# Attention output stored once in fp32 and split where it is used, and the recalled memory scaled behind the reads of the third score tile

## The chip, the cores and the metric

One core of a Trainium2 chip runs the whole program. The metric is device time in microseconds (us) from start to end of one execution; a kernel's time is the median of three runs.

## What is computed

Attention with a memory, then a gated MoE layer, all in fp32 (B 4, H 8, S 576, D 64; 2304 tokens, d 512, ff 1536):

```python
a = softmax(causal(q @ k.T / 8))
local = a @ v
mem_out = (phi(q) @ M_prev) / (phi(q) @ z_prev + 1e-6)      # phi(x) = elu(x) + 1
x = sigmoid(beta) * mem_out + (1 - sigmoid(beta)) * local     # 2304 x 512
out = (silu(x @ w_gate) * (x @ w_val)) @ w_out
```

## The kernel before

**Parts of fp32.** A matmul operand in fp32 is a sum of two fp32r tiles, a high part (a cast) and a low part (the number less its high part), and a product takes three matmuls: high x high, high x low, low x high. Where this text speaks of a split, it means a cast on ScalarE and a subtraction on VectorE or GpSimd.

**Attention** runs in iterations n = 0 to 16, one for each of the 16 (batch, pair of heads), the loop `for n in range(NP + 1)`. Iteration n computes scores, maxima and exponentials of pair n (`cur`) and the turned probabilities, the product with v and the memory part of pair n - 1 (`old`); it also splits q and k of pair n + 1 (`after`). Iteration 16 has no scores, it only finishes pair 15. Scores come in tiles of 128 queries t = 0 to 3 for each of two heads, and a last one of 64 queries for both (two halves of 288 keys, "the fourth-block scores"). All engines run in program order: the helper `queued` records every operation at L84 and ties it to the one before on its engine, so the order of the Python code is the order on each engine.

In an iteration VectorE reads the score tiles (`reading`, a custom reduction that adds a mask, scales, and takes the maximum `mx`; out tiles `ps` for t = 0, 1, `pl` for t = 2, 3, `p` for the last), makes the reciprocals `rs` of the sums `sm`, copies turned tiles (`g`), and scales the recalled memory: `mem = tr * w`, two operations in `recall`'s `scale()`. ScalarE computes the exponentials. GpSimd (`pool`) casts q and k of the next pair (`kh`, `qh`), makes their low parts (`ql`, `kl`), and multiplies the probabilities by `rs` and the gate `og`: four `ps`, four `pl` and one `p` for each pair, in `weighed`. A bank of scores is written again only when VectorE has read it.

At the end of an iteration the output of pair n - 1 stands in two PSUM tiles `tr`, 256 and 320 wide. `give` splits each out of PSUM: ScalarE casts it to `xh`, VectorE writes `xl = tr - xh`. The 256-wide one is done at the end of the iteration, the 320-wide one behind the first scores of the next; then two DMAs (`d2`) store `xh` and `xl` to DRAM, `xdh` and `xdl`. I call the start of the scores of iteration n boundary n. In iterations 3 to 15 three thirds of a weight matrix are prepared at the boundaries, one operation of VectorE each (from `EARLY` = 2, 6, 10): a clamp (`we`) at boundaries 4, 8, 12, a move (`wa`) at 5, 9, 13, a word (`wa`, two inputs of 512) at 6, 10, 14 and a low part (`wgl`, `wol`) at 7, 11, 15.

**MoE.** Tokens come in three blocks of 768 (`ORDER`), ff in 12 slices: 36 units. Each half block of x is 384 tokens. The first three units are plain (`eight`); the others take seven products in Strassen's manner (`seven`) from sums of quarters of x: `p1`, `p2`, `p4` and `p7`, `p6`, `p5`, `p3`, each with a high and a low tile `xp1h`, `xp1l` and so on. Products use two PSUM banks (`s`) in turn, so product n + 2 of a unit waits until VectorE or ScalarE has taken product n. `weigh` forms the products of gate and value, `zg` (i = 0) and `zh` (i = 1), and their splits `uh`, `ul`; `lower` multiplies the `u` of the unit before with w_out. `operands` prepares the weights of the next unit (`tt`, `bl`, `tl`). `plan[k]` lists what VectorE and ScalarE do behind product k of a unit. `sums(t0)` makes the sums of a block: it loads four quarters from `xdh` and `xdl` into `xr`, adds high and low (four additions 128x768), and forms s1, s and the two differences (four more). `direct` loads `p1`, `p2`, `p4` (for block 0 also `p7`) as they are, high and low, by DMA. For block 1 the sums stand in units 6 to 11 of block 0, for block 2 in units 9 to 11 of block 1.

Of the kernel before, what the change touches and what calls it, by code (L numbers as in the profile page):

```python
# [44 lines left out]
def attention_moe(ctx: ExitStack, tc: tile.TileContext, qt, kt_, v, m, beta, wg, wv, wo, out):  # L45
# [9 lines left out]
    xdh = dram.tile([128, NPAIR, NT], F32, name="xdh")  # L55
    xdl = dram.tile([128, NPAIR, NT], F32, name="xdl")
# [109 lines left out]
    xs = {p: [near.tile([128, 2, N2], F32R, name=f"x{p}{part}") for part in "hl"] for p in ("p1", "p2", "p7", "p4")}  # L166

# [88 lines left out]
    with tc.tile_pool(name="sb", bufs=1, reuse_waits="tile") as sb:  # L256
# [69 lines left out]
        class Pair:  # L326
# [181 lines left out]
            def give(self, t0, src):  # L508
                c = slice(t0 * 128, t0 * 128 + src.shape[1])
                act.copy(self.xh[:, c], src)  # L510
                return lambda: dve.tensor_tensor(self.xl[:, c], src, self.xh[:, c].bitcast(F32), op=ALU.subtract)

# [28 lines left out]
            def leave(self):  # L541
                first, rest = self.av
                self.xh = rot(sb, "xh", [128, 576], F32R, NX)
                self.xl = rot(sb, "xl", [128, 576], F32R, NX)
                self.give(0, first[:, 0:256])()

                def ending():
                    low = self.give(2, rest[:, 0:320])
                    return lambda: (low(), self.d2())

                return ending

            def d2(self):
                for dst, src in ((xdh, self.xh), (xdl, self.xl)):
                    SP.dma_start(dst[:, self.pr, self.b * S : self.b * S + S], src.bitcast(F32))
# [10 lines left out]
        ending = lambda: nothing  # L566
        copies = []
        for n in range(NP + 1):
# [10 lines left out]
            low = ending()  # L579
# [5 lines left out]
            low()  # L585
# [32 lines left out]
            scale()  # L618
# [6 lines left out]
            reads[0](1)  # L625
            if n == 0:
                one_less()
                scaled()
# [37 lines left out]
            ending = old.leave() if old else lambda: nothing  # L666
# [5 lines left out]
            for i, at in enumerate(EARLY):  # L672
                if n == at:
                    raw_top(act, i)
                if n == at + 1 and i < 3:
                    third_clamp(dve, i)
                if n == at + 2 and i < 3:
                    third_move(dve, i)
                if n == at + 3 and i < 3:
                    third_word(act, dve, i, copies)  # L680
                if n == at + 4 and i < 3:
                    low_part(dve)
            if n in AHEAD:
                raw_load(AHEAD.index(n), loads.get(n + 2))

        ending()()
# [7 lines left out]
    with tc.tile_pool(name="stg2", bufs=1, reuse_waits="tile") as stg2, \  # L694
# [47 lines left out]
        def block(x, t0, i, j):  # L742
            return x[:, 2 * j : 2 * j + 2, t0 + i * N2 : t0 + i * N2 + N2]

        def direct(t0, p, i, j):
            for dst, src in zip(xs[p], (xdh, xdl)):
                SP.dma_start(dst.bitcast(F32), block(src, t0, i, j))

        def sums(t0, here=False):

            got = rot(mbp, "xr", [128, 4, 2, N2], F32, 1)
            at = ((1, 0), (1, 1), (0, 0), (0, 1))
            a21, a22, a11, a12 = (got[:, n] for n in range(4))
            s1, s = (rot(mbp, name, [128, 2, N2], F32, 1) for name in ("xt", "xm"))
            tmp = (s, s1)
            mix = dict(p6=s, p7=a11, p5=s1, p3=a12)

            def load(n):
                for dst, src in ((got[:, n], xdh), (tmp[n % 2], xdl)):
                    ld = SP.dma_start(dst, block(src, t0, *at[n]))  # L760
                    follow(ld, last[DVE], "the loads that come before go first", mybir.DependencyClass.Sync)

            def add(n):
                if here:
                    h, l = (x.bitcast(F32) for x in xs[("p7", "p4", "p1", "p2")[n]])
                    dve.tensor_tensor(got[:, n], h, l, op=ALU.add)
                    return
                dve.tensor_tensor(got[:, n], got[:, n], tmp[n % 2], op=ALU.add)
                if n + 2 < 4:
                    load(n + 2)  # L770

            tt = lambda out, a, b, op: (lambda: dve.tensor_tensor(out, a, b, op=op))
            work = [lambda n=n: add(n) for n in range(4)] + [
                tt(s1, a21, a22, ALU.add), tt(s, s1, a11, ALU.subtract), tt(a12, a12, s, ALU.subtract),
                tt(a11, a11, a21, ALU.subtract),
            ]
            return lambda: (load(0), load(1)), work, mix
# [137 lines left out]
        first = units[0][0]  # L915
        for p, i, j in (("p1", 0, 0), ("p2", 0, 1), ("p7", 1, 0), ("p4", 1, 1)):
            direct(first, p, i, j)
# [5 lines left out]
        for n, unit in enumerate(units):  # L923
# [23 lines left out]
            if plain:  # L947
                if f == 0:
                    _, due, mix = sums(t0, True)
                    for k, some_ in enumerate(((0,), (1,), (2, 4), (3,))):  # L950
                        plan[k] += [due[i] for i in some_]
                if f == 1:
                    for k in range(3):
                        plan[k].append(due[5 + k])
                    for k, p in ((0, "p5"), (2, "p6")):
                        plan[k] += spreads(mix, ("h", p))
# [5 lines left out]
            if not end:  # L962
                follows = ORDER[ORDER.index(t0) + 1]
                if t0 == first and left in (5, 4, 3):
                    if left == 5:
                        begin, due, mix = sums(follows)
                        begin()
                    plan[5].append(due[5 - left])
                if not plain:
                    if left == 3 and t0 != first:  # L970
                        begin, due, mix = sums(follows)
                        plan[3].append(begin)
                    if left == 2:
                        for k, work in zip((5,), due[3:]) if t0 == first else zip((2, 4, 6), due):
                            plan[k].append(work)
                    if left == 1:
                        for k, work in zip((1, 3, 5), due[4:]) if t0 == first else zip((1, 2, 4, 6), due[3:]):
                            plan[k].append(work)
                    if left == 0:
                        plan[2].append(due[7])  # L980
                        plan[3] += spreads(mix, ("h", "p6"))
                        plan[4] += spreads(mix, ("l", "p6"), ("h", "p7"))
                        plan[6] += spreads(mix, ("l", "p7"))
                        arrive = [
                            (1, spreads(mix, ("h", "p5"))), (2, spreads(mix, ("l", "p5"))),
                            (3, spreads(mix, ("h", "p3"))), (4, spreads(mix, ("l", "p3"))),
                        ]
            down = [] if before is None else [
                lambda j=j, before=before: lower(*before, j) for j in (range(2 * nj) if n <= PLAIN else TURN)
# [3 lines left out]
            else:  # L993
                before = (unit, seven(ready.pop(n), down, plan, (0, 2, 4) if f else (3, 5, 6)))
            if not end and left == 0:
                direct(follows, "p1", 0, 0)
                direct(follows, "p2", 0, 1)
                direct(follows, "p4", 1, 1)
# [54 lines left out]
```

## Time and profile before

| what | value |
|---|---|
| time, median of 3 runs | 612.06 us (612.0 to 612.1) |
| profiled execution | 611.38 us, its span 609.6 us |
| TensorE (PE) busy | 599.6 us, 98% of the span |
| VectorE (DVE) busy | 485.0 us, 80% |
| ScalarE (ACT) busy | 395.2 us, 65% |
| GpSimd (POOL) busy | 214.8 us, 35%, nearly all of it in the attention |
| DMA | 102.46 MB, mean 168 GB/s |
| granted TensorE clock | 0.996 in the mean |

The profile is one execution; its engines are PE, DVE, ACT, POOL and SP (which issues the DMAs). A row of a timeline gives the start, the duration, the engine, L84 (the helper's line), the operation, the tile written and the tiles read, and in brackets how long the engine had stood idle and what ended that. The chain of waits follows the work that ended last back to the start. The attention lasts from 10 to about 190 us, the MoE from there to the end.

### The profile page before, as it was taken

How to read it: one execution, taken by the hardware profiler on the slowest of the kernel's cores; microseconds unless marked ns; L12 is line 12 of the kernel's file. 1: busy time of each engine (PE TensorE's matmuls, PEld its weight loads, DVE VectorE, ACT ScalarE, POOL GpSimd, SP SyncE). 2: the span in 40 equal slices, each digit the busy share in tenths (PEclk: the TensorE clock that was granted, in tenths of full speed). 3: DMA queues.
4: the chain of work that ended last, by engine and by line, in shares of the span. 5: the costliest groups of instructions: out<-in, count | busy, mean ns of one | idle time of the engine just before them, and what ended most of it. 6: DMA issues, size and time to landing. Idle time of an engine off the chain costs nothing.

```text
span 609.6 us, 11282 instructions
## 1 busy us (share of the span) xinstructions
PE 599.6 (98%) x3794; PEld 531.5 (87%) x3794; DVE 485.0 (80%) x1208; ACT 395.2 (65%) x917; POOL 214.8 (35%) x261
## 2 busy tenths in 40 slices
PE   6999999999999999999999999999999999999997
PEld 4878878778788999999899999999999999999996
DVE  6899999999988998898998665665888765665653
ACT  8788888888876777777656654454456654454442
POOL 7999999999963334334320000000000000000000
PEclk9999999999999999999999999999999999999999
DMA  8456756657337657799556622323755622332212
GB/s 250 133 159 178 255 171 204 215 179 216 141 117 277 187 182 239 239 361 282 192 175 208 217 92 70 112 96 115 232 184 177 211 100 69 107 103 69 70 35 103
DMA packets 49321, 102.46 MB, mean 168 GB/s; under 512 B 7024, under 2 KB 17136, under 8 KB 49264
## 3 DMA queue, kind: packets, MB, share of 16 engines
q1 hardware_dynamic: 48832, 101.32, 51.1%
q8 instruction: 30, 0.49, 0.3%
q10 hardware_dynamic: 432, 0.43, 0.2%
q14 instruction: 27, 0.22, 0.1%
HBM read 74.99 MB, written 26.74 MB: 167 GB/s over the span
## 4 chain that ended last, share of the span: by engine, by line
PE 96%; POOL 1%; DMA 1%; issue 0%; DVE 0%; ACT 0%; SPq 0%; ACTq 0%; DVEq 0%
PE s L84 60%; PE tr L84 36%; DMA qr<-in_qt_dram 1%; POOL ps L84 0%; POOL kl L84 0%; SPq L269 0%; ACT g L84 0%; POOL qh L84 0%; DVE rs L84 0%; ACT wa L84 0%; POOL pl L84 0%; DVE mem L84 0%; DVE pl L84 0%; SPq L560 0%; DVE pt L84 0%
## 5 line engine op out<-in xcount | busy, mean ns | idle before, releaser
L84 ACT ACTIVATE zh<-zh 128x384 f32<-128x384 f32 x33 | 17.4, 527 | 74.8 <-DVE zh L84 74.8
L84 POOL TENSOR_SCALAR pl<-pl,rs,og 128x384 f32<-128x384 f32 (+1 forms) x64 | 55.9, 886 | 9.4 <-DVE rs L84 9.4
L84 DVE TENSOR_TENSOR zv<-s,zv 128x384 f32<-128x384 f32 x33 | 18.4, 557 | 51.1 <-PE s L84 45.9
L84 PE MATMUL tr<-woh,ul 128*128 128x512 f32 x144 | 57.3, 398 | 0.0
L84 PE MATMUL tr<-woh,uh 128*128 128x512 f32 x144 | 57.0, 396 | 0.0
L84 PE MATMUL tr<-wol,uh 128*128 128x512 f32 x144 | 56.8, 394 | 0.0
L84 POOL TENSOR_SCALAR we<-we 128x512 f32<-128x512 f32 x32 | 24.9, 780 | 76.8 <-ACT we L84 76.7
L84 ACT ACTIVATE pl<-pl,mx 128x384 f32<-128x384 f32 (+1 forms) x64 | 42.3, 664 | 12.3 <-DVE mx L84 12.3
L84 PE MATMUL tr<-g,vp 128*64 128x320 f32 (+4 forms) x448 | 48.8, 360 | 0.3 <-ACT g L84 0.3
L84 DVE TENSOR_TENSOR tl<-tt,th 128x512 fp32r<-128x512 f32 x66 | 47.7, 723 | 0.0
L84 ACT CAST th<-tt 128x512 fp32r<-128x512 f32 x66 | 41.1, 622 | 9.6 <-DVE tt L84 6.3
L84 PEld LDWEIGHTS tr<-g,vp 128*64 128x64 f32 x448 | 29.4, 137 | 18.0 <-issue 2.3
L84 PE MATMUL s<-kh,qh 64*128 64x128 f32 (+4 forms) x160 | 37.2, 386 | 4.5 <-ACT kh L84 4.0
L84 ACT CAST uh<-zh 128x384 fp32r<-128x384 f32 x36 | 18.5, 513 | 32.6 <-DVE zh L84 32.3
L84 DVE TENSOR_TENSOR zg<-s,zp 128x384 f32<-128x384 f32 x33 | 18.4, 558 | 25.8 <-ACT bh L84 23.5
L84 DVE CUSTOM_DVE_ANT_0 pl<-s,maskp 128x384 f32<-128x384 f32 (+1 forms) x64 | 38.1, 615 | 0.3 <-PE s L84 0.3
L84 DVE TENSOR_TENSOR bl<-wr,bh 128x512 fp32r<-128x512 f32 x66 | 36.3, 550 | 0.0
L84 ACT CAST bh<-wr 128x512 fp32r<-128x512 f32 x66 | 33.9, 513 | 0.0
L84 PEld LDWEIGHTS tr<-woh,ul 128*128 128x128 f32 x144 | 27.1, 188 | 6.8 <-DVE ul L84 0.3
L84 ACT ACTIVATE ps<-ps,mx 128x128 f32<-128x128 f32 (+1 forms) x64 | 28.6, 453 | 6.4 <-DVE mx L84 6.4
L84 POOL TENSOR_SCALAR ps<-ps,rs,og 128x128 f32<-128x128 f32 (+1 forms) x64 | 32.0, 513 | 1.6 <-DVE rs L84 1.2
L84 DVE COPY g<-tr 128x384 f32<-128x384 f32 (+2 forms) x60 | 30.0, 518 | 2.7 <-PE tr L84 1.4
(198 smaller groups left out, 2000.4 us busy)
## 6 DMA issues: line engine op xcount, KB each, us to landing
wr<-wdr SPq DMA_DIRECT2D x24, 512.0 KB, 3.3
wraw<-in_wg_dram SPq DMA_DIRECT2D x12, 512.0 KB, 4.6
wraw<-in_wv_dram SPq DMA_DIRECT2D x12, 512.0 KB, 5.1
wraw<-in_wo_dram SPq DMA_DIRECT2D x12, 512.0 KB, 5.1
wol<-wdo SPq DMA_DIRECT2D x24, 256.0 KB, 2.8
woh<-wdo SPq DMA_DIRECT2D x24, 256.0 KB, 3.1
qr<-in_qt_dram SPq DMA_DIRECT2D x15, 384.0 KB, 3.2
vp<-in_v_dram SPq DMA_DIRECT2D x16, 320.0 KB, 4.1
```

What stands on the lines that cost most here:

```text
L84: ins = getattr(eng, name)(*args, **kw)
```

## The change

The output x is copied out of PSUM as fp32 by ScalarE (`xo`, 256 and 320 wide), and one DMA stores it to one DRAM tensor `xd`. VectorE has no `xl` any more. The four operands of block 0 that were loaded in parts are now loaded as fp32 into their low tiles at the ends of iterations 6, 8, 10 and 12 (`p1`, `p2`, `p7`, `p4`); in the iterations that follow ScalarE casts half of one to its high tile, and VectorE makes the low part in place, 128x384, one at each of the boundaries 9 to 16. `scale()` stands behind the two reads of tile t = 2. In the MoE `sums` loads four fp32 quarters and has four operations of 768 in place of eight; `p1`, `p2` and `p4` of blocks 1 and 2 are split in the last unit of the block before and in the first of their own. In `seven`, `weigh` takes i = 0 first except in the last unit, and `lower` takes its six tiles in the order 0 to 5 (before: 3, 4, 5, 0, 1, 2).

```diff
-    xdh = dram.tile([128, NPAIR, NT], F32, name="xdh")
-    xdl = dram.tile([128, NPAIR, NT], F32, name="xdl")
+    xd = dram.tile([128, NPAIR, NT], F32, name="xd")
...
+    where = dict(p1=(0, 0), p2=(0, 1), p7=(1, 0), p4=(1, 1))
+
+    def x_block(t0, i, j):
+        return xd[:, 2 * j : 2 * j + 2, t0 + i * N2 : t0 + i * N2 + N2]
...
-            def give(self, t0, src):
-                c = slice(t0 * 128, t0 * 128 + src.shape[1])
-                act.copy(self.xh[:, c], src)
-                return lambda: dve.tensor_tensor(self.xl[:, c], src, self.xh[:, c].bitcast(F32), op=ALU.subtract)
...
             def leave(self):
                 first, rest = self.av
-                self.xh = rot(sb, "xh", [128, 576], F32R, NX)
-                self.xl = rot(sb, "xl", [128, 576], F32R, NX)
-                self.give(0, first[:, 0:256])()
+                x = rot(sb, "xo", [128, 576], F32, NX)
+                act.copy(x[:, 0:256], first[:, 0:256])
 
                 def ending():
-                    low = self.give(2, rest[:, 0:320])
-                    return lambda: (low(), self.d2())
+                    act.copy(x[:, 256:576], rest[:, 0:320])
+                    SP.dma_start(xd[:, self.pr, self.b * S : self.b * S + S], x)
...
-            scale()
             if after and n:
                 after.lows()
...
             reads[0](0)
             reads[0](1)
+            scale()
...
+            for p, at in zip(("p1", "p2", "p7", "p4"), (6, 8, 10, 12)):
+                high, low = xs[p]
+                if n == at:
+                    SP.dma_start(low.bitcast(F32), x_block(ORDER[0], *where[p]))
+                for k in range(2):
+                    if n == at + 1 + k:
+                        act.copy(high[:, k], low[:, k].bitcast(F32))
+                    if n == at + 2 + k:
+                        dve.tensor_tensor(low[:, k], low[:, k].bitcast(F32), high[:, k].bitcast(F32), op=ALU.subtract)
...
+            def begin():
+                for n, at in enumerate(((1, 0), (1, 1), (0, 0), (0, 1))):
+                    SP.dma_start(got[:, n], x_block(t0, *at))
...
-        def seven(w, down, plan, away_at):
+        def seven(w, down, plan, away_at, final):
...
-            weigh(u, 1, g2, v2)
-            weigh(u, 0, g1, step(6, "p3", False))
+            ps = step(6, "p3", False)
+            for i, g, v in ((1, g2, v2), (0, g1, ps)) if final else ((0, g1, ps), (1, g2, v2)):
+                weigh(u, i, g, v)
...
+                if left == 3:
+                    begin, due, mix = sums(follows)
+                    plan[3].append(begin)
+                if left == 1:
+                    plan[2].append(due[0])
+                    plan[5].append(due[1])
+                if left == 0:
+                    plan[1] += spreads(mix, ("h", "p1"))
+                    plan[2] += spreads(mix, ("l", "p1"), ("h", "p2"))
+                    plan[3] += [due[2]] + spreads(mix, ("l", "p2"), ("h", "p6"))
+                    plan[4] += spreads(mix, ("l", "p6"), ("h", "p7")) + [due[3]]
+                    plan[6] += spreads(mix, ("l", "p7"))
+                    arrive = [
+                        (0, spreads(mix, ("h", "p5"))), (1, spreads(mix, ("l", "p5"), ("h", "p4"))),
+                        (2, spreads(mix, ("l", "p4"), ("h", "p3"))), (3, spreads(mix, ("l", "p3"))),
+                    ]
...
-                lambda j=j, before=before: lower(*before, j) for j in (range(2 * nj) if n <= PLAIN else TURN)
+                lambda j=j, before=before: lower(*before, j) for j in range(2 * nj)
```

Three places show how the order moves. The first is VectorE at boundary 9, before (`ISA` is a read of a score tile, or of its maximum):

```order
L84 TENSOR_TENSOR rs_279<-sm_152,tiny 128x1
L84 RECIPROCAL rs_279<-rs_279 128x1
L84 TENSOR_TENSOR xl_567<-tr_298,xh_566 128x256
L84 TENSOR_SCALAR wa_1453<-wraw_1015 128x512
L84 ISA ps_271,mx_255<-s_161,maskp 128x128
L84 ISA mx_255 128x1
L84 ISA ps_273,mx_255<-s_162,maskp 128x128
L84 ISA mx_255 128x1
L84 TENSOR_TENSOR xl_567<-tr_303,xh_566 128x320
L84 ISA ps_275,mx_255<-s_153,maskp 128x256
```

and with the change:

```order
L83 TENSOR_TENSOR rs_278<-sm_151,tiny 128x1
L83 RECIPROCAL rs_278<-rs_278 128x1
L83 TENSOR_SCALAR wa_1430<-wraw_999 128x512
L83 TENSOR_TENSOR xp1l<-xp1l,xp1h 128x384
L83 ISA ps_270,mx_254<-s_160,maskp 128x128
L83 ISA mx_254 128x1
L83 ISA ps_272,mx_254<-s_161,maskp 128x128
L83 ISA mx_254 128x1
L83 ISA ps_274,mx_254<-s_152,maskp 128x256
```

Both `xl` are gone, and a split from two SBUF tiles stands behind the weight operation and ahead of the first read. The second place is VectorE in the middle of the same iteration, before:

```order
L84 TENSOR_TENSOR rs_319<-sm_256,tiny 128x4
L84 RECIPROCAL rs_319<-rs_319 128x4
L84 TENSOR_TENSOR mem_309<-tr_286,w_310 128x384
L84 TENSOR_TENSOR mem_309<-tr_291,w_310 128x256
L84 ISA pl_344,mx_255<-s_161,maskp 128x384
L84 ISA mx_255 128x1
L84 ISA pl_346,mx_255<-s_162,maskp 128x384
L84 ISA mx_255 128x1
L84 COPY g_258<-tr_303 128x4x128
```

and with the change:

```order
L83 TENSOR_TENSOR rs_318<-sm_255,tiny 128x4
L83 RECIPROCAL rs_318<-rs_318 128x4
L83 ISA pl_341,mx_254<-s_160,maskp 128x384
L83 ISA mx_254 128x1
L83 ISA pl_343,mx_254<-s_161,maskp 128x384
L83 ISA mx_254 128x1
L83 TENSOR_TENSOR mem_308<-tr_285,w_309 128x384
L83 TENSOR_TENSOR mem_308<-tr_290,w_309 128x256
L83 COPY g_257<-tr_302 128x4x128
```

The two memory scalings have moved behind the reads; `rs` stands where it was. The third place is VectorE in the last unit of block 0, from the weights' low part to the taking of the sixth product (`zh`), before:

```order
L84 TENSOR_TENSOR bl_2907<-wr_2811,bh_2906 128x512
L84 TENSOR_TENSOR xr_2587<-xr_2587 128x768
L84 TENSOR_TENSOR wol_2807<-wa_2040,woh_2806 128x512
L84 TENSOR_TENSOR tl_2905<-tt_2786,th_2904 128x512
L84 TENSOR_TENSOR tt_2786<-wr_2811,tt_2786 128x256
L84 TENSOR_TENSOR zv_2909<-s_154,zv_2909 128x384
L84 TENSOR_TENSOR bl_2907<-wr_2811,bh_2906 128x256
L84 TENSOR_TENSOR xp6l<-xm_2589,xp6h 128x384 x2
L84 TENSOR_TENSOR zh_2742<-s_153,zh_2742 128x384
```

and with the change:

```order
L83 TENSOR_TENSOR bl_2868<-wr_2772,bh_2867 128x512
L83 TENSOR_TENSOR xp1l<-xr_2548,xp1h 128x384 x2
L83 TENSOR_TENSOR wol_2768<-wa_2015,woh_2767 128x512
L83 TENSOR_TENSOR tl_2866<-tt_2747,th_2865 128x512
L83 TENSOR_TENSOR tt_2747<-wr_2772,tt_2747 128x256
L83 TENSOR_TENSOR xr_2548<-xr_2548 128x768
L83 TENSOR_TENSOR xp2l<-xr_2548,xp2h 128x384 x2
L83 TENSOR_TENSOR zv_2870<-s_153,zv_2870 128x384
L83 TENSOR_TENSOR bl_2868<-wr_2772,bh_2867 128x256
L83 TENSOR_TENSOR xp6l<-xm_2550,xp6h 128x384 x2
L83 TENSOR_TENSOR xr_2548<-xr_2548,xm_2550 128x768
L83 TENSOR_TENSOR zh_2703<-s_152,zh_2703 128x384
```

Five operations more stand ahead of `zh` here: the two low parts of `p1`, the two of `p2`, and a second operation of 768.

## Rows read from the trace of the kernel before

**Rows 1.** The page: GpSimd's line in the 40 slices, and the chain by engine.

```profile
POOL 7999999999963334334320000000000000000000
...
PE 96%; POOL 1%; DMA 1%; issue 0%; DVE 0%; ACT 0%; SPq 0%; ACTq 0%; DVEq 0%
```

**Rows 2.** Waits of POOL from 52 to 170 us: total, times, longest.

```profile
POOL pl L84 <- DVE rs L84: 4.5, 11, 0.4
```

**Rows 3.** Timeline of POOL, iterations 8 and 9.

```profile
95.37 0.67 POOL L84 TENSOR_SCALAR kh<-kr 128x576 fp32r<-128x576 f32 x1
...
100.18 1.45 POOL L84 TENSOR_TENSOR kl<-kr,kh 128x576 fp32r<-128x576 f32 x1
102.04 3.46 POOL L84 TENSOR_SCALAR pl<-pl,rs,og 128x384 f32<-128x384 f32 x4 [0.41 <-DVE rs L84]
```

**Rows 4.** Timeline of DVE and ACT, the same iterations.

```profile
95.82 0.23 DVE L84 TENSOR_TENSOR rs<-sm,tiny 128x4 f32<-128x4 f32 x1
...
96.18 0.86 DVE L84 TENSOR_TENSOR mem<-tr,w 128x384 f32<-128x384 f32 x2
...
101.06 0.19 ACT L84 ACTIVATION_READ_ACCUMULATOR pl<-pl,mx 128x1 f32 x1
...
101.29 0.36 DVE L84 TENSOR_TENSOR rs<-sm,tiny 128x4 f32<-128x4 f32 x1
...
103.10 0.44 DVE L84 TENSOR_SCALAR wa<-wraw 128x512 int32<-128x512 int32 x1
103.47 0.28 DVE L84 CUSTOM_DVE_ANT_0 ps<-s,maskp 128x128 f32<-128x128 f32 x1
```

**Rows 5.** Timeline of POOL and DVE at boundaries 3, 10 and 2.

```profile
35.89 3.24 POOL L84 TENSOR_SCALAR pl<-pl,rs,og 128x384 f32<-128x384 f32 x4 [0.41 <-DVE rs L84]
...
112.90 3.73 POOL L84 TENSOR_SCALAR pl<-pl,rs,og 128x384 f32<-128x384 f32 x4 [0.41 <-DVE rs L84]
...
24.31 1.53 DVE L84 SCALAR_TENSOR_TENSOR ph<-qe,ph 128x640 f32<-128x640 f32 x2
...
24.57 3.88 POOL L84 TENSOR_SCALAR pl<-pl,rs,og 128x384 f32<-128x384 f32 x4 [0.50 <-DVE rs L84]
```

**Rows 6.** Windows: 14 stretches; start:end, length, busy time by engine.

```profile
52.85:54.56 1.71, 1.71 (x16) 1.71 (x15) 1.70 (x6) 1.15 (x4) 1.71 (x4) 1.00 0.47 82
...
sum 26.00, PE 25.74 PEld 24.64 DVE 25.99 ACT 16.11 POOL 25.59; mean PE 1.84 PEld 1.76 DVE 1.86 ACT 1.15 POOL 1.83
```

**Rows 7.** The chain in order of time, MoE: start, length, what.

```profile
273.80 4.52 PE s L84 x24
...
285.53 4.52 PE s L84 x24
...
325.83 2.08 PE s L84 x12
...
337.31 2.08 PE s L84 x12
```

**Rows 8.** Waits of the whole span: TensorE's weight loads on `zg`.

```profile
PEld s L84 <- DVE zg L84: 1.4, 5, 0.3
```

**Rows 9.** Timeline of DVE, last unit of block 0.

```profile
316.54 0.56 DVE L84 TENSOR_TENSOR zg<-s,zp 128x384 f32<-128x384 f32 x1 [0.28 <-PE s L84]
...
319.15 0.95 DVE L84 TENSOR_TENSOR xr<-xr 128x768 f32<-128x768 f32 x1
320.02 0.68 DVE L84 TENSOR_TENSOR wol<-wa,woh 128x512 fp32r<-128x512 f32 x1
...
322.75 1.03 DVE L84 TENSOR_TENSOR xp6l<-xm,xp6h 128x384 fp32r<-128x384 f32 x2
323.69 0.55 DVE L84 TENSOR_TENSOR zh<-s,zh 128x384 f32<-128x384 f32 x1
```

**Rows 10.** Timeline of DVE and POOL, iteration 3.

```profile
40.53 0.75 DVE L84 TENSOR_TENSOR rs<-sm,tiny 128x4 f32<-128x4 f32 x1
...
41.67 1.97 POOL L84 TENSOR_SCALAR ps<-ps,rs,og 128x128 f32<-128x128 f32 x4 [0.40 <-ACT ph L84]
```

More of the change, by code (lines that the diff above doesn't have):

```diff
@@ L565, in attention_moe @@
         nothing = lambda *args: None
-        ending = lambda: nothing
+        ending = nothing
         copies = []
@@ L578, in attention_moe @@
                 old.turns()
-            low = ending()
+            ending()
             while copies:
@@ L584, in attention_moe @@
             reads[0](1)
-            low()
             if n == 0:
@@ L665, in attention_moe @@
                     cur.weighed(((4, 0),))
-            ending = old.leave() if old else lambda: nothing
+            ending = old.leave() if old else nothing
             if n + 2 < NP:
@@ L682, in attention_moe @@
                     low_part(dve)
+            for p, at in zip(("p1", "p2", "p7", "p4"), (6, 8, 10, 12)):
[7 more added lines that the diff above has]
+                        dve.tensor_tensor(low[:, k], low[:, k].bitcast(F32), high[:, k].bitcast(F32), op=ALU.subtract)
             if n in AHEAD:
                 raw_load(AHEAD.index(n), loads.get(n + 2))
-        ending()()
+        ending()
         low_part(dve)
@@ L740, in attention_moe, with sums @@
             xs[p] = [mbp.tile([128, 2, N2], F32R, name=f"x{p}{part}") for part in "hl"]
[L742 to L749, printed above, removed]
+        def sums(t0):
             got = rot(mbp, "xr", [128, 4, 2, N2], F32, 1)
-            at = ((1, 0), (1, 1), (0, 0), (0, 1))
             a21, a22, a11, a12 = (got[:, n] for n in range(4))
             s1, s = (rot(mbp, name, [128, 2, N2], F32, 1) for name in ("xt", "xm"))
[L755 to L770, printed above, removed]
-            tt = lambda out, a, b, op: (lambda: dve.tensor_tensor(out, a, b, op=op))
[L773 to L777, printed above, removed]
+            mix = dict(p1=a11, p2=a12, p6=s, p7=a11, p5=s1, p4=a22, p3=a12)
+            def begin():
+                for n, at in enumerate(((1, 0), (1, 1), (0, 0), (0, 1))):
+                    SP.dma_start(got[:, n], x_block(t0, *at))
+            tt = lambda out, a, b, op: (lambda: dve.tensor_tensor(out, a, b, op=op))
+            return begin, [
+                tt(s1, a21, a22, ALU.add), tt(s, s1, a11, ALU.subtract),
+                tt(a11, a11, a21, ALU.subtract), tt(a12, a12, s, ALU.subtract),
+            ], mix
         def high(mix, p, k):
@@ L915, in attention_moe @@
         first = units[0][0]
-        for p, i, j in (("p1", 0, 0), ("p2", 0, 1), ("p7", 1, 0), ("p4", 1, 1)):
-            direct(first, p, i, j)
         before = None
@@ L948, in attention_moe @@
                 if f == 0:
-                    _, due, mix = sums(t0, True)
-                    for k, some_ in enumerate(((0,), (1,), (2, 4), (3,))):
-                        plan[k] += [due[i] for i in some_]
+                    begin, due, mix = sums(t0)
+                    begin()
+                    plan[2].append(due[0])
+                    plan[3].append(due[1])
                 if f == 1:
[L953 to L956, printed above, removed]
+                    for k, i, p in ((0, 2, "p5"), (2, 3, "p6")):
+                        plan[k] += [due[i]] + spreads(mix, ("h", p))
                         plan[k + 1] += spreads(mix, ("l", p))
@@ L963, in attention_moe @@
                 follows = ORDER[ORDER.index(t0) + 1]
[L964 to L987, printed above, removed]
@@ new lines, in attention_moe @@
+                if left == 3:
+                    begin, due, mix = sums(follows)
+                    plan[3].append(begin)
+                if left == 1:
+                    plan[2].append(due[0])
+                    plan[5].append(due[1])
[9 more added lines that the diff above has]
+                    ]
@@ L993, in attention_moe @@
             else:
[L994 to L998, printed above, removed]
+                before = (unit, seven(ready.pop(n), down, plan, (0, 2, 4) if f else (3, 5, 6), n == len(units) - 1))
         halves()
```

3 lines of the change are left out of this document (removed).

## The prediction

> **What bounds the kernel now.** I read the chain of waits first. It puts 96% of the span on TensorE and 1% on GpSimd [rows 1], so everything seems to be worth what it takes from TensorE. In the MoE that holds: a Strassen unit takes 11.48 us from one chain row to the same row of the next unit where nothing stalls [rows 7], and TensorE issues without a gap. For the attention I did not trust it, because the line of GpSimd in the 40 slices stands at 9, 90% or more, through the whole attention [rows 1]. So the second view was GpSimd's own waits between 52 and 170 us: 4.5 us in all, 11 times, each 0.4 [rows 2]. An engine with slack would wait longer in some iterations than in others. GpSimd waits the same 0.41 once in each iteration and is busy for the rest.
>
> The third view, the timeline of iterations 8 and 9, says why. The first `pl` scaling needs the `rs` that VectorE makes from the sums of the exponentials. ScalarE reads out the last sum at 101.06, for 0.19 us, and VectorE's addition starts at 101.29. It then takes 0.36 us, till 101.65, and GpSimd's `kl` subtraction (100.18, 1.45 us) ends at 101.63 [rows 3, 4]. In the middle of the iteration the same happens: the addition at 95.82 takes 0.23 us, and GpSimd's `kh` (95.37, 0.67 us) ends at 96.04 [rows 3, 4]. I read this as a lock: a VectorE instruction with two SBUF inputs waits for a running GpSimd instruction. GpSimd starts again only 0.41 us after its own `kl`, however early the sums were there. So GpSimd paces itself, and an earlier TensorE cannot shorten its round: from `pl` to `pl` it is 112.90 - 102.04 = 10.86 us in iteration 9 [rows 3, 5].
>
> TensorE is tied to that round twice. After `rs` in mid-iteration come the two memory scalings (0.86 us) and only then the two reads of the third score tile, whose banks the fourth-block scores (`s` 128x288) want [rows 4]. After `kl` come `rs`, `ph`, `xl`, a weight operation and the first `ps` read at 103.47, on which the first exponential of the iteration hangs [rows 4].
>
> **The change, part by part.** Sums are made against the profiled execution, 611.38 us; it lies 0.68 below the median of 612.06, and I carry the difference over to the median.
>
> *Reads ahead of the memory scaling.* The 14 stretches from the third tile's transposes to the end of the fourth-block scores take 26.00 us, the shortest 1.71 [rows 6]. If all came down to that, the gain would be 26.00 - 14 x 1.71 = 2.1 us. That is the upper end; the lower is nothing, since an earlier TensorE meets the same `kl` and the same `rs` at the next iteration. One thing GpSimd itself gets: in iteration 3 the `rs` addition came at 40.53, with GpSimd's `qh`, was held for 0.75 us, and GpSimd then stood for 0.40 us (its row names ScalarE, but what `ps` needs is `rs`) [rows 10]. With iteration 2's stretch shorter by some 0.3 us, `rs` falls into `kh` and ends with it. I take **-0.4**. The two scalings now lie behind the reads, ahead of the `g` copy: VectorE has the same work done by then, and `mem` is wanted over 1 us later, so they cost nothing; without that cover it would be up to 0.86 us per iteration.
>
> *`xl` goes, the split of `p1`, `p2`, `p7`, `p4` comes.* The old `xl` read PSUM and one SBUF tile. The 256-wide one stood ahead of the weight operation, which starts at 103.10 [rows 4], when GpSimd's first `pl` is through; without `xl` it would wait for that. So removing it gives **0** (at best 0.15 in iterations 7, 11 and 15, where the 320-wide one frees a bank late). The new low parts are 128x384 with both inputs in SBUF, one at each of the boundaries 9 to 16, directly behind the weight operation where there is one, ahead of the `ps` reads. What they cost GpSimd I take from its four `pl` scalings: 3.24 us with no weight operation, 3.46 beside a clamp or move, 3.73 beside a 512-wide operation with two inputs [rows 3, 5]. So 0.22 and 0.49 more. Two `ph` back to back (24.31, 1.53 us) made them 3.88, 0.64 more than one [rows 5]: VectorE kept GpSimd out through both. A 384-wide subtraction takes 0.47 us of VectorE (two: 322.75 to 323.69) [rows 9]. Its price for GpSimd lies between 0.37 (0.49 x 384/512, by width) and 0.47 (all of it, right behind another). I take 0.43, nearer the upper end, since at boundaries 9 to 14 all six stand right behind a weight operation. Boundaries 9 to 14 each lengthen the round: 6 x 0.43 = **+2.6** (ends 0 and 2.8). The Trainium skill, page "SBUF — State Buffer", section "Who interferes with whom", states that such an instruction and one of GpSimd that reads SBUF contend for shared ports, that whoever issues first has them for the whole instruction, and that issue order decides who is blocked. By that rule GpSimd, which waits already, would go ahead of the second of two operations, as in the third rival, and the sum would be +5.3 instead of +3.5; the row with two `ph` is against it. Boundary 15 has no round behind it; it delays the first `ps` read by 0.47 - 0.34 of the `xl` in its place, and up to 0.3 through the chain behind it: **+0.3**. The eight high casts on ScalarE fall into its wait for TensorE at the boundary: nothing; the store becomes one DMA of the same bytes as either of the two: nothing.
>
> *MoE, block 0.* Five units take 11.73 us (285.53 - 273.80) instead of 11.48 (337.31 - 325.83) [rows 7], because TensorE waits for VectorE's `zg`, five times, 1.4 us by the waits [rows 8], behind a 768-wide addition that no longer exists. 5 x 0.25 less the overlap of one: **-1.15** (ends -1.4 and -0.9).
>
> *MoE, from block 0 to block 1.* In the last unit VectorE already works without a gap from `zg` (316.54) to `zh` (323.69) [rows 9]. The change puts four 384-wide splits (4 x 0.47) and one more 768-wide operation (320.02 - 319.15 = 0.87) ahead of `zh` there. That is 2.75; I take off 0.35 for short waits on ScalarE there that the added work fills, so `zh` moves to 323.69 + 2.4 = 326.1 and ends 0.55 later, while the next unit wants its bank at 325.83 [rows 7]: 0.8, and 0.25 for the last product of the unit, whose bank `zv` frees, also later. Behind it `zg`, `zh` and two `xp7l` stand ahead of `ul`, some 0.6 more of waiting: **+1.65** (ends 0.5 and 2.3). From block 1 to 2 `wa` and `wol` (up to 0.68 each [rows 9]) are gone, so little shows: **+0.3** (0 to 0.9).
>
> *MoE, start.* Block 0's four loads now stand in SP's queue among the weight loads, and the first sum waits for them: **+0.2** (0 to 1).
>
> The sum is -0.4 + 0 + 2.6 + 0.3 - 1.15 + 1.65 + 0.3 + 0.2 = +3.5: 611.38 + 3.5 = 614.9 for a profiled execution, **615.6 us** for the median.
>
> **The rivals.** *TensorE is the pace after all* (the other side): the fourth-block scores start earlier and every stretch goes to 1.71. Then -2.1, and at seven boundaries some 0.2 for the later `ps` read, +1.4, with the MoE's +1.0: 612.4, no change; with VectorE catching up at the block transition as well (-1.65), 610.7, faster. For it speaks the chain of waits [rows 1]; against it, that GpSimd's wait is the same in every iteration [rows 2]. It decides if GpSimd's wait falls below 0.4 or its round below 10.8. Chances 0.12 and 0.10, some of the latter with gains I have not seen.
>
> *The new splits do not hold GpSimd* (they find it in a gap, or lock nothing at this width): 615.6 - 2.6 = 613.0, no change. Against it speak the two `rs` [rows 4]. 0.16.
>
> *GpSimd slips in between the weight operation and the split.* What is known is that VectorE kept its place through two `ph` [rows 5]; if here GpSimd's waiting `pl` goes first, the split and the reads behind it wait out a scaling of some 0.5 us, `rs` comes after `kl`, and each of six boundaries costs 0.3 more: 615.6 + 1.8 = 617.4. 0.12.
>
> **How the numbers follow.** A measurement here can tell about 0.2%, 1.2 us, from no change. The forecast (GpSimd is the pace, splits held against it) has 0.50, nearly all of it slower; with the slipping GpSimd 0.62 slower, 0.26 within 0.2%, 0.12 faster. The range runs from 611.0, between the first rival's two times, to 617.8, the last rival with the MoE's start 0.4 later still; so it leaves out most of the second of those times and little above. The forecast's own range is 613.5 to 617.0, from the ends of the two transitions (-1.45, +0.65), of the splits (6 x 0.37 = 2.2 at the least, where they do hold GpSimd) and of the start.
>
> **What would show it.** Right: GpSimd still waits about 0.41 each iteration, its rounds from iteration 9 on are longer by about 0.4 and those before 9 are as before; its `pl` group rises to about 3.9 and 4.2; the stretches go to 1.7 and TensorE's gain reappears as waits at the boundary; the five stalls are gone; TensorE waits for `zh` at the first unit of block 1. Wrong: rounds before 9 shorter by 0.15, or `pl` groups that stay at 3.46 and 3.73.

## The result, and the profile after

The changed kernel takes 614.75 us (median of 6 runs, 614.43 to 616.06) against 612.03 us for the kernel before (6 runs, 611.23 to 612.21). The ratio is 1.0051, 95% interval 1.0038 to 1.0064: slower by 2.3 to 3.9 us. The forecast was 615.6 us and slower; the time lies in the range, 0.85 us below that number.

The page of the changed kernel, GpSimd's line in the 40 slices and the chain by engine, answers to [rows 1]:

```profile
POOL 6999999999974424424410000000000000000000
...
PE 92%; DVE 4%; ACT 2%; DMA 1%; issue 0%; ACTq 0%; POOL 0%; DVEq 0%
```

GpSimd is still busy 90% or more of the attention, and the chain still hides it; what is new there is 4% on VectorE and 2% on ScalarE. GpSimd's waits from 52 to 170 us answer to [rows 2] (total, times, longest):

```profile
POOL pl L83 <- ACT p L83: 3.3, 8, 0.4
POOL pl L83 <- DVE rs L83: 0.8, 2, 0.4
```

That is 4.1 us in 10 waits, 0.41 each as before. In eight of them the row names ScalarE's `p`, which this scaling does not read. At boundary 9 the exponentials that it reads are done by 101.01, and it starts 0.18 us behind the reciprocal `rs` (102.05), as before (0.17): what GpSimd stands for is `rs`. The timeline of VectorE and GpSimd at boundaries 9 and 10 answers to [rows 3 to 5]:

```profile
100.40 1.43 POOL L83 TENSOR_TENSOR kl<-kr,kh 128x576 fp32r<-128x576 f32 x1
...
101.14 0.70 DVE L83 TENSOR_TENSOR rs<-sm,tiny 128x4 f32<-128x4 f32 x1
...
102.23 3.78 POOL L83 TENSOR_SCALAR pl<-pl,rs,og 128x384 f32<-128x384 f32 x4 [0.40 <-ACT p L83]
...
102.95 0.63 DVE L83 TENSOR_SCALAR wa<-wraw 128x512 int32<-128x512 int32 x1
103.50 0.54 DVE L83 TENSOR_TENSOR xp1l<-xp1l,xp1h 128x384 fp32r<-128x384 f32 x1
103.97 0.28 DVE L83 CUSTOM_DVE_ANT_0 ps<-s,maskp 128x128 f32<-128x128 f32 x1
...
113.41 4.04 POOL L83 TENSOR_SCALAR pl<-pl,rs,og 128x384 f32<-128x384 f32 x4 [0.41 <-DVE rs L83]
```

The sums are ready earlier (`rs` starts at 101.14, 0.69 ahead of `kl`'s end at 101.83), and all that this buys is a longer wait: the addition again ends with `kl`, at 101.84. The split follows the weight operation without a gap, GpSimd stays out through both, and its four scalings take 3.78 and 4.04 us where they took 3.46 and 3.73 [rows 3, 5].

The 14 stretches that the moved reads were to shorten, all of them, answer to [rows 6]:

```profile
52.91:54.62 1.71, 1.71 (x16) 1.71 (x15) 1.71 (x7) 1.57 (x6) 1.71 (x5) 1.00 0.49 85
...
sum 24.08, PE 24.08 PEld 24.08 DVE 24.08 ACT 22.59 POOL 23.89; mean PE 1.72 PEld 1.72 DVE 1.72 ACT 1.61 POOL 1.71
```

The move did there what it says, 26.00 to 24.08 us. TensorE spends the gain, and with it what the splits add to GpSimd's round, at the next boundary, as the waits of its weight loads from 100 to 172 us show; in the same list of the kernel before the first of these has 0.4 in all and the second does not stand, and in e1 below, without the splits, they have 0.4 and 0.9:

```profile
PEld tr L83 <- ACT g L83: 2.0, 6, 0.3
PEld tr L83 <- POOL pl L83: 1.9, 6, 0.5
```

In the MoE, the chain's rows of two units of block 0 lie 11.48 us apart (before 11.73, [rows 7]), and three waits of TensorE's weight loads stand at the transition to block 1, two at that to block 2:

```profile
269.59 5.56 PE s L83 x30
...
281.07 5.56 PE s L83 x30
```

```profile
325.28 0.19 PEld L83 LDWEIGHTS s<-xp3h,bh 128*128 128x128 f32 x1 [0.47 <-DVE zv L83]
...
327.88 0.19 PEld L83 LDWEIGHTS s<-xp1h,bh 128*128 128x128 f32 x1 [1.03 <-DVE zh L83]
...
330.82 0.19 PEld L83 LDWEIGHTS s<-woh,ul 128*128 128x128 f32 x1 [0.52 <-DVE ul L83]
...
466.22 0.19 PEld L83 LDWEIGHTS s<-xp1h,bh 128*128 128x128 f32 x1 [0.35 <-DVE zh L83]
...
469.16 0.19 PEld L83 LDWEIGHTS s<-woh,ul 128*128 128x128 f32 x1 [0.52 <-DVE ul L83]
```

To see where time went, each trace is cut at the same events: the first scores of iterations 2, 9 and 15, and the first products of MoE units 0, 11, 13, 23 and 25 (us; units 13 to 22 take 114.80 everywhere and are left out). Both kernels were traced twice.

| trace | it. 2 starts | it. 2-8 | it. 9-14 | it. 15, 16 | units 0-10 | 11, 12 | 23, 24 | 25 to end |
|---|---|---|---|---|---|---|---|---|
| before | 25.47 | 77.25 | 66.08 | 18.93 | 126.31 | 23.11 | 22.96 | 134.68 |
| before, second (e10) | 25.63 | 77.12 | 66.03 | 18.93 | 126.30 | 23.11 | 22.96 | 134.68 |
| changed | 26.55 | 75.91 | 67.99 | 19.51 | 125.39 | 24.52 | 23.52 | 134.81 |
| changed, second (e11) | 25.49 | 75.82 | 67.81 | 19.50 | 125.91 | 24.52 | 23.54 | 134.80 |
| e1, reads alone | 25.35 | 76.56 | 66.15 | 18.98 | 126.32 | 23.09 | 22.96 | 134.69 |
| e2, scaling back | 26.85 | 77.68 | 67.80 | 19.20 | 126.37 | 24.52 | 23.53 | 134.80 |
| e3, no low parts | 24.75 | 75.82 | 65.72 | 18.82 | 125.95 | 24.51 | 23.53 | 134.79 |
| e4, low behind reads | 24.85 | 76.05 | 67.26 | 19.05 | 126.39 | 24.51 | 23.54 | 134.80 |
| e5, weigh alone | 25.76 | 78.17 | 65.92 | 18.92 | 125.41 | 22.96 | 22.96 | 134.68 |
| e6, kh on ScalarE | 25.92 | 75.77 | 66.68 | 19.00 | 126.16 | 24.53 | 23.55 | 135.01 |
| e7, respread | 25.05 | 75.87 | 67.83 | 19.50 | 125.31 | 24.23 | 23.25 | 134.79 |
| e8, reads, weigh, kh | 25.80 | 75.98 | 65.85 | 18.76 | 125.41 | 22.96 | 22.96 | 134.69 |
| e9, kh but for words | 24.96 | 75.61 | 64.97 | 18.99 | 125.40 | 22.96 | 22.96 | 134.70 |

The start of iteration 2 moves between 24.75 and 26.85 us from execution to execution, with no order by kernel; the first trace of the changed kernel has a late one. From the second trace of before to the second of the changed kernel the pieces add up to -0.14 - 1.30 + 1.78 + 0.57 - 0.39 + 1.41 + 0.58 + 0.12 = +2.6, the 2.7 us of the medians.

### The profile page after: what moved, and what is told of

Same layout as the page of the kernel before. It is cut to its first block, busy times and chain, and to the rows that moved or that the text cites. A ratio compares the mean times of both kernels' runs of the same rounds, so it can differ in the third digit from the quotient of the medians.

```text
span 613.0 us, 11207 instructions
## 1 busy us (share of the span) xinstructions
PE 599.8 (98%) x3794; PEld 531.6 (87%) x3794; DVE 474.9 (77%) x1184; ACT 401.7 (66%) x937; POOL 218.5 (36%) x261
## 4 chain that ended last, share of the span: by engine, by line
PE 92%; DVE 4%; ACT 2%; DMA 1%; issue 0%; ACTq 0%; POOL 0%; DVEq 0%
PE s L83 57%; PE tr L83 35%; ACT g L83 1%; ACT ps L83 1%; DMA kr<-in_kt_dram 1%; DVE xr L83 0%; DVE zg L83 0%; DVE xp6l L83 0%; DVE xp7l L83 0%; DVE zh L83 0%; DVE tl L83 0%; DVE tt L83 0%; DVE xp2l L83 0%; DVE bl L83 0%; DVE pl L83 0%
## 5 line engine op out<-in xcount | busy, mean ns | idle before, releaser
L83 POOL TENSOR_SCALAR pl<-pl,rs,og 128x384 f32<-128x384 f32 (+1 forms) x64 | 58.1, 921 | 9.8 <-DVE rs L83 5.3
L83 POOL TENSOR_SCALAR we<-we 128x512 f32<-128x512 f32 x32 | 26.7, 836 | 73.4 <-ACT we L83 73.1
L83 ACT CAST uh<-zg 128x384 fp32r<-128x384 f32 x36 | 18.5, 514 | 37.9 <-DVE zg L83 37.8
L83 DVE SCALAR_TENSOR_TENSOR zg<-s,zg 128x384 f32<-128x384 f32 x36 | 20.0, 556 | 17.4 <-PE s L83 17.4
L83 ACT COPY g<-tr 128x384 f32<-128x384 f32 (+1 forms) x60 | 29.9, 523 | 5.6 <-ACT g L83 5.0
L83 DVE TENSOR_TENSOR zh<-s,zh 128x384 f32<-128x384 f32 x33 | 18.4, 556 | 18.6 <-PE s L83 18.5
```

The lines of the kernel that those rows point to most:

```text
L83: ins = getattr(eng, name)(*args, **kw)
```

## The experiments

The theory: GpSimd is the pace of the attention, and the new splits cost what they keep it out. The rival: TensorE is the pace, and the splits cost by the later `ps` reads. The first four runs tell these apart.

**e1, the reads alone**, in the kernel before:

```diff
-            scale()
             if after and n:
                 after.lows()
...
             reads[0](0)
             reads[0](1)
+            scale()
```

> The kernel before with one part of the change: the memory scaling behind the reads of tile 2. If GpSimd is the pace, TensorE can only use up its lead on GpSimd (scores start 0.7 us behind the first pl scaling before, 0.25 with the change) and save GpSimd's 0.4 in iteration 3: about -0.9, 611.1 us; the rounds of iterations 8 to 14 stay at 10.88 and 11.14 within 0.05, and GpSimd waits 0.41 each time. If TensorE is the pace, all 14 stretches go to 1.71: -2.1, 609.9 us, rounds shorter by 0.15 each to the end of the attention.

Measured 610.41 us against 612.31, ratio 0.9973 (0.9964 to 0.9982), so 1.1 to 2.2 us faster: by its time, between the two numbers, the run does not decide. Its trace does. All stretches go to 1.72:

```profile
sum 24.15, PE 24.15 PEld 24.14 DVE 24.15 ACT 23.43 POOL 23.93; mean PE 1.72 PEld 1.72 DVE 1.72 ACT 1.67 POOL 1.71
```

and yet iterations 9 to 14 take 66.15 us, as much as before, while 2 to 8 fall from 77.25 or 77.12 to 76.56. The gain is a lead used up once and one iteration, not 14 stretches; GpSimd waits 4.5 us in 11 times, as in [rows 2]. The rest of the timed gain I trace to a thing seen in e2 and e5, below.

**e2, the scaling back ahead of the reads**, in the changed kernel, the reverse of that diff.

> The changed kernel with the scaling back ahead of the reads. If GpSimd is the pace: the lead and iteration 3's 0.4 are lost, +0.9, 615.7 us, and the rounds 9 to 14 stay within 0.05 of the changed kernel's 11.25 and 11.45. If TensorE is the pace: +2.1, 616.9 us, with the rounds 9 to 14 longer by 0.15.

Measured 616.0 us, ratio to before 1.0065 (1.005 to 1.0079). Iterations 9 to 14 take 67.80, as in the second trace of the changed kernel. Where the reads stand makes no difference to them.

**e3, without the eight low subtractions** (what they compute is left out):

```diff
-                    if n == at + 2 + k:
-                        dve.tensor_tensor(low[:, k], low[:, k].bitcast(F32), high[:, k].bitcast(F32), op=ALU.subtract)
```

> The changed kernel without the eight low subtractions of the attention (the low tiles of block 0 keep the whole x, so this part of the computation is left out). If their cost is that they hold GpSimd: rounds 9 to 14 fall by 0.31 each, the pl groups from 3.78 and 4.05 to about 3.39 and 3.65, and the time by 1.9 to 2.3 us to about 612.7. If they cost through the later ps reads alone: the pl groups stay, TensorE's waits at the boundary go, 7 x 0.2 = 1.4, 613.3 us. If they cost nothing: 614.7.

Measured 611.07 us, ratio 0.9983 (0.9973 to 0.9992), 1.6 us below the lowest number expected. Against the second trace of the changed kernel iterations 9 to 14 lose 2.09 us and the last two 0.68, together more than the 1.9 to 2.3 expected; another 0.74 of the 3.5 us between the two traces is an earlier start of iteration 2, which scatters. GpSimd's scalings at boundary 9:

```profile
100.33 3.38 POOL L83 TENSOR_SCALAR pl<-pl,rs,og 128x384 f32<-128x384 f32 x4 [0.41 <-ACT p L83]
```

3.38 where they take 3.78 with the split: 0.40 for one subtraction, which 6 rounds pass on. It falls on the second of the four scalings, in the changed kernel and in e3:

```profile
103.29 1.21 POOL L83 TENSOR_SCALAR pl<-pl,rs,og 128x384 f32<-128x384 f32 x1
```

```profile
101.38 0.82 POOL L83 TENSOR_SCALAR pl<-pl,rs,og 128x384 f32<-128x384 f32 x1
```

The splits do hold GpSimd. 3.38 is also 0.08 below the 3.46 of before: without `xl` the weight operation waits at the lock already when GpSimd's first scaling ends, and is through 0.27 us behind that end (before 0.43).

**e4, the subtractions behind the four `ps` reads**:

```diff
...
+            while late_low:
+                late_low.pop(0)()
...
-                        dve.tensor_tensor(low[:, k], low[:, k].bitcast(F32), high[:, k].bitcast(F32), op=ALU.subtract)
+                        late_low.append(lambda low=low, high=high, k=k: dve.tensor_tensor(low[:, k], low[:, k].bitcast(F32), high[:, k].bitcast(F32), op=ALU.subtract))
```

> The changed kernel with the same eight subtractions behind the four ps reads, so that the reads come 0.47 us earlier and GpSimd meets the subtraction one scaling later. If GpSimd's round is what counts, nothing is gained: 614.4 to 614.9 us, rounds 9 to 14 within 0.1 of the changed kernel's. If the later reads are what counts: -1.4 to -1.9, about 613.0 us.

Measured 613.04 us, ratio 1.0013 (1.0005 to 1.0022): the rival's number, and 1.4 us below the least that GpSimd's round alone would give. The trace says how much of that is the rival's. The scalings take

```profile
100.66 3.67 POOL L83 TENSOR_SCALAR pl<-pl,rs,og 128x384 f32<-128x384 f32 x4 [0.41 <-ACT p L83]
```

so the same subtraction costs GpSimd 0.29 here, not 0.40. Against e11 iterations 9 to 14 are 0.55 us shorter and the last two 0.45; iteration 2 starts 0.64 earlier, iterations 2 to 8 are 0.23 longer, and 0.48 is lost in unit 1. So in this place too most of GpSimd's share of the cost stays, and the place decides on a quarter of it and on what boundary 15 loses, 1.0 us together. That much of the rival is right; what lies above 1.0 in the timed gain of 1.7 to the changed kernel is not shown to be its doing.

**e5, weigh's order alone**, with the order of `lower` that goes with it, in the kernel before (the additions of 768 stay):

```diff
...
-            weigh(u, 1, g2, v2)
-            weigh(u, 0, g1, step(6, "p3", False))
+            ps = step(6, "p3", False)
+            for i, g, v in ((1, g2, v2), (0, g1, ps)) if final else ((0, g1, ps), (1, g2, v2)):
+                weigh(u, i, g, v)
...
-                lambda j=j, before=before: lower(*before, j) for j in (range(2 * nj) if n <= PLAIN else TURN)
+                lambda j=j, before=before: lower(*before, j) for j in range(2 * nj)
...
```

> The kernel before with one part of the change: weigh takes i = 0 first (but in the last unit) and lower goes 0 to 5; the 768-wide additions stay. If zg was late because zh stood ahead of it, 0.47 us, its move is enough for a stall of 0.25: all five units fall to 11.48, -1.15, and TensorE does not wait for zg any more. If only the removal of the additions helps, the units stay at 11.73 and the time is that of the kernel before.

Measured 611.31 us, ratio 0.9989 (0.998 to 0.9998). The first stalled unit falls to 11.48, the next three to 11.51 and 11.52, and units 11 and 12 take 22.96, 2 x 11.48: -1.05 of the -1.15 expected. The order alone does it (the two orders were not run apart). This trace also has three iterations (3 to 5) of 11.3 to 11.4 us, where both of before have one. Its timeline in iteration 4:

```profile
52.22 0.75 DVE L84 TENSOR_TENSOR rs<-sm,tiny 128x4 f32<-128x4 f32 x1
```

```profile
53.36 1.95 POOL L84 TENSOR_SCALAR ps<-ps,rs,og 128x128 f32<-128x128 f32 x4 [0.40 <-ACT ph L84]
```

It is [rows 10] again: `rs` comes as `qh` starts (52.23), and GpSimd stands for 0.40. e2 has three such iterations too; no trace with the reads ahead of the scaling has one (the wait alone comes back in e6, e8 and e9, see e8). In the four traces with the old order there are 1, 1, 3 and 3 of them, at some 0.5 us each. That fits the timed gain of e1, 1.9, being larger than the 0.7 between single traces; it is not shown for the timed runs, which have no traces.

**e6, `kh` on ScalarE**, in the changed kernel, to take work from GpSimd:

```diff
-ACT_K = (0, 1)
+ACT_K = tuple(range(16))
```

> The changed kernel with the cast kh on ScalarE in all iterations (before only in two), which takes 0.65 us out of every round of GpSimd and puts some 0.55 us on ScalarE ahead of the first exponential. If GpSimd is the pace of rounds 9 to 14: they fall from 11.25 and 11.45 to 10.7 to 10.9, -2.5 to -3.5 us, about 611.7; GpSimd waits more than 0.41. If it is the chain through VectorE and ScalarE at the boundary: no gain, or up to 0.5 us slower per iteration, 614.7 to 620.

Measured 612.38 us, ratio 1.0002 (0.9993 to 1.0011), 2.4 us below the changed kernel. Iterations 4, 5, 7 and 8 take 10.65 to 10.66, the least that any iteration takes in any trace; I take it for TensorE's own time. 9 and 11 to 13 take 10.74 to 10.97, where they took 11.15 to 11.48. Iterations 6, 10 and 14 take 11.57 to 11.65: there the word's cast and `kh` both stand on ScalarE ahead of the first exponential. So between the traces iterations 9 to 14 fall by 1.1 to 1.3 us in sum, where 2.5 to 3.5 were expected. A second reason shows in e8.

**e7, a transition spread out**, in the changed kernel: `p7`'s low parts and the last sum go into the first unit of the next block, block 0's first sum stands one product later.

```diff
-                    plan[2].append(due[0])
-                    plan[3].append(due[1])
+                    plan[3] += [due[0], due[1]]
...
-                    plan[4] += spreads(mix, ("l", "p6"), ("h", "p7")) + [due[3]]
-                    plan[6] += spreads(mix, ("l", "p7"))
+                    plan[4] += spreads(mix, ("l", "p6"), ("h", "p7"))
...
-                        (0, spreads(mix, ("h", "p5"))), (1, spreads(mix, ("l", "p5"), ("h", "p4"))),
+                        (0, spreads(mix, ("l", "p7"), ("h", "p5"))), (1, spreads(mix, ("l", "p5"), ("h", "p4")) + [due[3]]),
```

> The changed kernel with three operations of a block transition put later: the low parts of p7 and the last sum (768 wide) into the first unit of the next block, and block 0's first sum one product later. If VectorE's work ahead of zh and ul is what stalls the first unit, 1.74 us less stand there: units 11 and 12 fall from 12.54 and 11.98 to about 11.7 and 11.5, the second transition from 11.56 and 11.97 to 11.48 both, -1.8 us; the stall behind block 0's first sum (0.1 to 1.0) goes too: 612.3 to 612.9. If TensorE waits for something else there, the units stay.

Measured 612.55 us, ratio 1.0012 (1.0003 to 1.0021). Unit 11 falls from 12.54 to 11.78, but unit 12 rises from 11.98 to 12.45. Its weight loads:

```profile
325.23 0.19 PEld L83 LDWEIGHTS s<-xp1h,bh 128*128 128x128 f32 x1 [0.17 <-DVE zh L83]
...
331.82 0.19 PEld L83 LDWEIGHTS s<-xp5h,th 128*128 128x128 f32 x1 [0.47 <-ACT zh L83]
...
335.93 0.19 PEld L83 LDWEIGHTS s<-xp3h,bh 128*128 128x128 f32 x1 [0.80 <-DVE zv L83]
```

The wait for `zh` falls from 1.03 to 0.17 and that for `ul` is gone, so it was VectorE's work ahead of them; but in the next unit VectorE has three pairs of low parts already, and the moved work makes `zv` late there. Units 0 to 10 take 125.31: with the first sum later, nothing waits for it. The time lies in the expected range, but by luck: the two transitions give 0.6 us of the 1.8 expected, the first sum 0.1 to 0.6, and the rest of the 2.2 us to the changed kernel is not shown.

**e8, a version from the parts that pay**: the kernel before with e1's and e5's edits and `kh` on ScalarE; x is stored in two parts as it was.

> The kernel before, with x stored in two parts as it was, with the reads ahead of the scaling, weigh's new order and kh on ScalarE. If GpSimd is the pace of the attention: its rounds fall by 0.65, TensorE comes to its own 10.7 a round: -0.7 - 1.15 and some 3 us, about 607.3 us. If TensorE or the boundary chain is the pace: -0.7 - 1.15 and nothing from kh, 610.4 us or more.

Measured 608.96 us, ratio 0.9947 (0.9935 to 0.9959). GpSimd's waits from 52 to 170 us:

```profile
POOL ps L84 <- DVE rs L84: 5.9, 11, 0.9
POOL pl L84 <- DVE rs L84: 5.3, 11, 0.8
```

It now waits twice in each iteration, mostly 0.40 ahead of `ps` and 0.41 ahead of `pl`. The first of these is not slack, but [rows 10] again: with `kh` gone the `rs` of mid-iteration meets `qh` and ends with it, at 95.45 in iteration 8, and GpSimd stands for 0.40:

```profile
94.73 0.72 POOL L84 TENSOR_SCALAR qh<-qr 128x640 fp32r<-128x640 f32 x1
95.84 0.45 POOL L84 TENSOR_SCALAR ps<-ps,rs,og 128x128 f32<-128x128 f32 x1 [0.40 <-DVE rs L84]
```

```profile
95.09 0.36 DVE L84 TENSOR_TENSOR rs<-sm,tiny 128x4 f32<-128x4 f32 x1
```

So of the 0.67 us that `kh` takes out of a round, 0.40 come back as a wait. Iterations 8, 9, 12 and 13 take 10.65 to 10.66, from 10.87 to 10.91, and GpSimd's rounds in them (from `pl` to `pl`) 10.59 to 10.63, from 10.86 to 10.91: there the two engines come out level, and GpSimd has hardly any slack. An order of `rs` and `qh` without this wait was not run. Iterations 6, 10 and 14 take 11.58 to 11.81, and in them GpSimd waits 0.9 ahead of `ps`. Against e1 the attention from iteration 2 on is 1.1 us shorter, where some 3 were expected, and the time stayed 1.7 above the expectation.

**e9**, e8 with `kh` left on GpSimd for the pairs 7, 11 and 15, whose cast would meet the word's:

```diff
-ACT_K = tuple(range(16))
+ACT_K = tuple(n for n in range(16) if n not in (7, 11, 15))
```

> The version before this one (reads ahead, weigh's order, kh on ScalarE), with kh left on GpSimd for pairs 7, 11 and 15, whose cast meets the word's cast on ScalarE. If the 11.6 to 11.8 us of iterations 6, 10 and 14 come from the two casts ahead of the first exponential: they fall to about 11.1 and the time by 1.5 us, to 607.4. If GpSimd is the pace of those rounds too: they stay above 11.3, and nothing is gained.

Measured 607.46 us, ratio 0.9928 (0.9914 to 0.9942). Iterations 6, 10 and 14 fall to 11.23, 11.02 and 11.07; 7 and 11, in front of which GpSimd has the cast again, rise from 10.71 to 10.91 and 10.92. This is the fastest version: 4.6 us below the kernel before, 7.3 below the changed one.

**e10 and e11**, both kernels traced once more.

> The kernel before once more, for a second trace. If the scatter of its times (610.4 to 613.3) comes from the start and from iterations in which rs meets qh: the scores of iteration 2 start between 24.7 and 26.9, the number of iterations 3 to 6 at 11.3 to 11.4 differs from the first trace's one, and those without stay at 10.75 to 10.87 and 11.14; rounds 7 to 14 and the MoE's units are the same within 0.03.

> The changed kernel once more, for a second trace. The start of iteration 2 between 24.7 and 26.9 (26.55 in the first trace), no iteration 3 to 5 above 10.9, rounds 9 to 14 at 11.15 to 11.25 and 11.45, unit 1 of the MoE between 12.6 and 13.6, units 11 and 12 at 12.5 and 12.0.

611.38 and 613.99 us. Before: one iteration of 11.34, the others within 0.05 of the first trace's (the expectation of a different number fell), units the same. Changed: iteration 2 starts at 25.49, 1.06 earlier; iterations 9 to 14 take 11.12 to 11.46; unit 1 takes 13.11 where the first trace has 12.59, because VectorE's first sum waits longer, 2.94 against 2.49 us (the rows name no cause; in e7, one product later, the row names block 0's load `xr<-xd`); units 11 and 12 are the same.

## Why the prediction was right, and where not

*GpSimd as the pace* is shown: shorter stretches alone leave iterations 9 to 14 where they were (e1), their return changes nothing (e2), and a GpSimd without `kh` lets iterations 8, 9, 12 and 13 come down to 10.65 (e8), though 0.40 of its 0.67 us come back as a wait.

*Reads ahead of the scaling, -0.4.* Measured in iterations 2 to 8: -1.3. The step took only iteration 3's wait. It left out that TensorE can use up its lead once: scores start 0.73 us behind the first `pl` scaling at boundary 10 before, 0.30 with the change (113.71 against 113.41). And "`xl` goes, 0" left out the 0.08 that GpSimd gains at each weight operation. Of the 1.3, e1 shows 0.6 to 0.7 for the reads; the 0.08 at five weight operations make some 0.4, and the rest is not accounted for. So the rounds before 9 are not "as before". The prediction had named rounds there that are shorter by 0.15 as a sign of being wrong: GpSimd's in iterations 4 to 8 are shorter by 0.07 to 0.10 (first traces; in e1, where `xl` stays, by 0.05 at most), but TensorE's iterations 2 to 8 by 0.19 in the mean. And the 10.8 below which GpSimd's round was to speak for TensorE as the pace is passed by a little, 10.77 in iterations 4 and 5 of e11; that is the 0.08 again, since e1 has 10.86 and 10.85 there.

*The splits, 6 x 0.43 = +2.6.* Measured in iterations 9 to 14: +1.8 to +1.9. One costs GpSimd 0.40 (e3), of which the 0.08 come off; the term was mis-sized by that and the mechanism holds. The eight casts, put at nothing, cost nothing that shows: e3 has them, and its iterations 9 to 14 are shorter than before (65.72 against 66.08). GpSimd did not slip in between: at boundary 9 its second scaling stands from 103.29, the split starts at 103.50, within the weight operation (102.95 to 103.58), and the scaling ends at 104.50, 0.46 behind the split. So the reading of the Trainium skill, page "SBUF — State Buffer", section "Who interferes with whom", on which the third rival rested, that the engine waiting longer goes first, does not show here: VectorE's second operation came later than GpSimd's scaling and went ahead of it. That VectorE and GpSimd exclude each other for whole instructions does agree: `rs` takes 0.70 us at boundary 9, to the end of `kl`.

*Boundary 15, +0.3.* Measured +0.57 for the last two iterations, 0.68 with e3 as the reference: under-sized, as it left out that TensorE also waits for the second `pl` scaling there. The split at boundary 16 has no term in the sum; against e3 all that the two iterations lose has come by 3 us behind boundary 15, so it cost nothing.

*Block 0, -1.15.* The size holds (four units of -0.25, and 0.15 in unit 11), the reason does not: "behind a 768-wide addition that no longer exists". e5 keeps the additions and loses the stalls by weigh's order (with that of `lower`). Either may be enough; the additions' removal without the new order was not run.

*First transition, +1.65.* The waits of the weight loads are 0.47 (`zv`, forecast 0.25), 1.03 (`zh`, forecast 0.8) and 0.52 (`ul`, forecast 0.6); in part they lie under products that still run (at 327.88 TensorE itself stands for 0.60), so that units 11 and 12 take 24.52, 1.56 above two units and 1.41 above before, which had 0.15 of the old stall there. *Second, +0.3:* +0.57, since `ul` is 0.52 late there too and I had counted on `wa` and `wol` only. *Start, +0.2:* 0.07 and 0.59 in two traces.

In sum 3.5 forecast, 2.6 measured: 0.9 less from iterations 2 to 8 and 0.8 less from the splits, against which boundary 15, the start of the MoE, the second transition and 0.12 in the last unit, which was not followed up, came out higher. That the time lies within 0.9 us of the forecast is in part luck: terms 1.7 us too high stand against others 1.1 too low.

## What to carry to other kernels

An engine that waits the same short time in every round, and has no other wait, can set the pace even where the chain of waits gives it 1%, as here; an earlier engine beside it then gains its lead once and no more. Before moving VectorE work from a PSUM source to two SBUF sources, count what it takes from GpSimd and not only what it takes from VectorE. Where an iteration has the same total on several engines, the gain lies in taking work from the one without slack: here one cast moved to ScalarE, but for the rounds in which ScalarE has a cast already. Read the waits again after such a step: here the cast that went had covered a second wait, 0.40 us a round.

## What the runs showed that I had not expected

The start of iteration 2 scatters by 2.1 us over the 13 traces (24.75 to 26.85 us), by 1.06 between the two of the changed kernel. And the lock has a bad phase: an `rs` that meets the start of `qh` is held for 0.75 us and GpSimd then stands for 0.40, in one to three iterations in a row in traces of the old order, and in nearly every iteration once `kh` no longer stands ahead of `qh` (e6, e8, e9; `rs` itself is held more briefly there, for 0.36 us in iteration 8 of e8). Placing a 0.47 us subtraction a few reads later took its price for GpSimd from 0.40 to 0.29.
